# Exponentials read from an SBUF copy of the scores, with scores three steps ahead and four copy buffers

## The chip, the core and the metric

One core of a Trainium2 chip runs the whole program. The metric is device time in microseconds (us), median of the runs, lower is better. Engines: PE is TensorE, DVE is VectorE, ACT is ScalarE, POOL is GpSimd, SP is SyncE. PE accumulates in PSUM, which DVE and ACT read; everything else lies in SBUF.

## The reference, cut to what matters

The part around the change is an attention over clusters, for 2 batches of 8 heads, 768 rows, head width 64:

```python
q_assign = np.argmax(np.einsum('bhsd,hcd->bhsc', q_n, c_n), axis=-1)
k_assign = np.argmax(np.einsum('bhsd,hcd->bhsc', k_n, c_n), axis=-1)
mask = q_assign[:, :, :, None] == k_assign[:, :, None, :]
scores = scale * np.matmul(q, k.transpose(0, 1, 3, 2))
scores = np.where(mask, scores, -1000000000.0)
scores = scores - np.max(scores, axis=-1, keepdims=True)
attn = np.exp(scores)
attn = attn / (np.sum(attn, axis=-1, keepdims=True) + 1e-09)
return np.matmul(attn, v).astype(np.float32)
```

Its output passes a low-rank mix over the tokens with a feed-forward block (512 to 2048 to 512), and then a second block (512 to 1024, a convolution of width 3 as a gate, back to 512). Those follow the attention and are not touched.

## The kernel before

The attention is a software pipeline of 96 steps, one for each tile of 128 query rows by 768 keys (6 tiles to a head, 12 steps to a pair of heads, 8 pairs). `step(n)` is a list of calls, and each engine executes its instructions in exactly the order in which they are called. In step n before the change:

- PE: `s_mm(n + 2)` writes the scores of tile n+2 into a PSUM buffer `sc` (two buffers), in a first part (L351, q and k split in two terms for precision) and a second part (L362, which adds the mask through 16 one-hot rows of `cd`). Then come `pv_mm` of an earlier head (L405, every other step), work for the next pair (below), and `t_mm(n)`, six transposes of the exponentials `e` of tile n (L389) into two PSUM tiles `tr`. `tr`, the one-hot tiles and the mixing tiles share a ring of three PSUM buffers.
- ACT: `t_out(n - 1, 0)` copies one `tr` tile to SBUF (L396), then `s_exp(n + 1)` (L380) makes `e` of tile n+1 from `sc`, with the row's bias `nb` and the row sum.
- DVE: `t_out(n - 1, 1)` copies the other `tr` tile, then `s_max(n + 2)` (L368) reads `sc`, writes the scores times -SCALE into the SBUF tile `e`, and gets their row minimum `nb` out of the same pass. What it writes into `e` is not used: the exponential overwrites it. `e` has three buffers.

For each next pair of heads, PE computes similarities (`sims_wide`, L214) and turns them (`sims_turn`, L228); five DVE operations make the one-hot rows (L245, L247, L249, L251, L253; L249 and L253 have both inputs in SBUF); PE transposes them (`onehot_t`, L260), ACT evicts them and SP puts them into `cd`. POOL loads the operands of a coming head by three DMAs (`load_ops`, L113 to L115) and subtracts (`split_ops`, L125 and L126, both inputs in SBUF). The operand tiles `ab` and `cd` have three buffers for three heads in turn, so that L113, when it loads a head, waits for the last `s_mm` of the head three before. POOL takes all this in its own order too: L113 to L115, then a piece of a weight job (L534, L538 or L515), the small sum L694, L125, L126.

Before the loop, `warm` issues matmuls on zeros; the first steps have no `pv_mm`, and PE waits there for the second half of q's split (`split_first(1, "q")`, whose POOL part is L200). When all heads of batch 0 are done, `mix_t` (step 8 of a pair) brings in eight ACT casts and four DVE subtractions in turn, and its tile too takes a buffer of the PSUM ring.

Of the kernel before, what the change touches and what calls it, by code (L numbers as in the profile page):

```python
# [21 lines left out]
AF = mybir.ActivationFunctionType  # L22
# [11 lines left out]
def tile_kernel(ctx: ExitStack, tc: tile.TileContext, qk, vv, cen, u_w, v_w, w1, w2, win, wout, conv, out):  # L34
    nc = tc.nc
# [3 lines left out]
    NT = S // P  # L39
    HS = S // 2  # L40
# [10 lines left out]
    SCALE = 1.0 / float(D) ** 0.5  # L51
# [15 lines left out]

    att = ExitStack()
    acon = att.enter_context(tc.tile_pool(name="acon", bufs=1))
    a_e = att.enter_context(tc.tile_pool(name="a_e", bufs=3))  # L70
    a_pt = att.enter_context(tc.tile_pool(name="a_pt", bufs=2))
    a_s = att.enter_context(tc.tile_pool(name="a_s", bufs=6))
    a_v = att.enter_context(tc.tile_pool(name="a_v", bufs=2))
# [7 lines left out]
    scores = ExitStack()  # L81
# [69 lines left out]
    def warm(count):  # L151
        for _ in range(count):
            nc.tensor.matmul(idle, busy[:, 0:P], busy, start=True, stop=True)
# [54 lines left out]
    def sims_wide(b, p):  # L208

        pw = ps_t.tile([P, HS], F32, tag="t", name="simw")  # L210
        for half in range(2):
            for i, (r, cb) in enumerate(zip(raw[b, p], (cbq, cbk))):
                o = 2 * NC * (2 * half + i)
                nc.tensor.matmul(pw[o:o + 2 * NC], cb[:, p], r[:, half * HS:(half + 1) * HS], start=True, stop=True)  # L214
        ohst[b, p] = {"pw": pw}

    def sims_copy(b, p):
        sw = a_oh.tile([P, HS], F32, tag="sw", name="sw")
        nc.scalar.copy(sw, ohst[b, p].pop("pw"))
        ohst[b, p]["sw"] = sw  # L220
# [34 lines left out]
    def onehot_t(b, p):  # L255
        oh = ohst[b, p]["oh"]
        pt = ps_t.tile([4 * NC, S], BF16, tag="t", name="oht")
        for t in range(NT):
            g0 = 8 * (t % (NT // 2)) + 4 * (t // (NT // 2))
            nc.tensor.transpose(pt[:, t * P:(t + 1) * P], oh[:, g0:g0 + 4].rearrange("p g c -> p (g c)"), identb)  # L260
        ohst[b, p]["pt"] = pt
# [73 lines left out]
    NQ = B * H * NT  # L335
    NHEAD = B * H
    st = {}
    X = {}

    def head_of(n):  # L340
        b, r = divmod(n, H * NT)
        h, t = divmod(r, NT)
        return b, h, t

    def s_mm_ab(n):
        b, h, t = head_of(n)
        ab, _ = ops[b, h]
        ps = ps_s.tile([P, 2, 512], F32, tag="s", name="sc")
        c0 = t * P
        for f in range(2):  # L350
            nc.tensor.matmul(ps[:, f, 0:HS], ab[:, 0, c0:c0 + P], ab[:, 1, f * HS:(f + 1) * HS], start=True, stop=False)  # L351
        st["s", n] = ps

    def s_mm(n):
        b, h, t = head_of(n)
        if ("s", n) not in st:
            s_mm_ab(n)
        ps = st["s", n]
        _, cd = ops[b, h]
        c0 = t * P  # L360
        for f in range(2):
            nc.tensor.matmul(ps[:, f, 0:HS], cd[0:80, 0, c0:c0 + P], cd[0:80, 1, f * HS:(f + 1) * HS], start=False, stop=True)  # L362

    def s_max(n):
        ps = st["s", n]
        nb = a_s.tile([P, 1], F32, tag="nb", name="nb")
        e = a_e.tile([P, 2, HS], F32, tag="e", name="e")
        nc.vector.tensor_scalar(  # L368
            out=e, in0=ps[:, :, 0:HS], scalar1=-SCALE, scalar2=3e38, op0=ALU.mult, op1=ALU.min, accum_out=nb,
        )  # L370
        st["nb", n] = nb
        st["e", n] = e

    def s_exp(n):
        ps = st.pop(("s", n))
        nb = st.pop(("nb", n))
        if n % NT == 0:
            st["sum", n // NT] = a_s.tile([P, NT], F32, tag="sum", name="sum", bufs=4)
        e = st["e", n]
        nc.scalar.activation(e, ps[:, :, 0:HS], AF.Exp, scale=SCALE, bias=nb, accum_out=st["sum", n // NT][:, n % NT:n % NT + 1])  # L380

    NK = NT // 2

# [14 lines left out]
    def pv_mm(g, k):  # L398

        b, h, _ = head_of(NT * g)  # L400
        if k == 0:
            st["pv", g] = ps_pv.tile([P, HS], F32, tag="pv", name="pv")
        acc, pt = st["pv", g], st["pt", g]
        for i in range(2):
            nc.tensor.matmul(  # L405
                acc[i * D:(i + 1) * D], vts[b, h // 2][:, h % 2, k], pt[:, k, i * NK:(i + 1) * NK].rearrange("p a b -> p (a b)"),
                start=(k == 0), stop=(k == NT - 1),
            )
        if k == NT - 1:
            st.pop(("pt", g))  # L410
# [142 lines left out]
    def mix_t(b):  # L553

        def mm():
            pt = ps_t.tile([P, P], F32, tag="t", name="mt")
            for t in range(NT):
                for c in range(ND):
                    nc.tensor.matmul(
                        pt[c * R:(c + 1) * R], uw[:, t], X[b][:, t, c * P:(c + 1) * P], start=(t == 0), stop=(t == NT - 1))  # L560
            return pt

        def evac(pt):
            for c in range(ND):
                src, cs = pt[c * R:(c + 1) * R], slice(c * P, (c + 1) * P)
                nc.scalar.copy(tts[b][0:R, cs], src)
                nc.vector.tensor_sub(tts[b][R:2 * R, cs], src, tts[b][0:R, cs])
                nc.scalar.copy(tts[b][2 * R:3 * R, cs], src)  # L568

        return mm, evac  # L570
# [30 lines left out]
    def mix_rest(b):  # L601
        for t in range(NT):
            mixing.append(mix_u(b, t))
        for t in range(NT):
            (mixing if b * NT + t < TG or b > 0 else later).append(mix_x(b, t))
# [28 lines left out]

    PLAN = ({2 * k: (2 * k, 2 * k + 1) for k in range(NK)}, NT - 2), ({k: (2 * k, 2 * k + 1) for k in range(NK)}, NK - 1)
    MIX_AT = (4, 6, 8, 10)

    SIM_AT, TURN_AT, ONEHOT_AT, ROWS_AT = 0, (2, 4), ((2, 2, 3, 3, 4), (4, 4, 5, 5, 6)), (5, 7)

    def step(n):  # L640
        pair, s = divmod(n, 2 * NT)
        mix = None
        if s == 8 and pair > 0 and n < NQ:
            b, p = divmod(pair - 1, NP)
            if p == NP - 1:
                mixing.append(mix_t(b))
                mix_rest(b)
        if n == 0:
            sims_wide(0, 1)
            warm(7)  # L650
        if n + 2 < NQ:
            s_mm(n + 2)
        ahead = divmod(pair + 1, NP)
        wide = 0 <= n < NQ and 1 < pair + 1 < B * NP
        rows = 0 <= n < NQ and pair + 1 < B * NP and s == ROWS_AT[pair == 0]
        turn = 0 <= n < NQ and pair + 1 < B * NP and s == TURN_AT[pair == 0]
        if rows:
            onehot_t(*ahead)

        g, r = divmod(n - NT - 1, NT)  # L660
        ks, last = PLAN[g == NHEAD - 1]
        if 0 <= g < NHEAD:
            for k in ks.get(r, ()):
                pv_mm(g, k)
        done = g - 1 if r == 0 else g if g == NHEAD - 1 and r == last + 1 else -1
        if 0 <= done < NHEAD - (r == 0):
            fin_t(done)
        elif mixing and (s in MIX_AT or pair == B * NP - 1):
            mix = mixing.pop(0)
            got = mix[0]()  # L670
        if s == SIM_AT and wide:
            sims_wide(*ahead)
        if turn:
            sims_turn(*ahead)
        if 0 <= n < NQ:
            t_mm(n)
        if 0 <= n - 1 < NQ:
            for i in range(2):
                t_out(n - 1, i)
        if 0 <= n + 1 < NQ:  # L680
            s_exp(n + 1)
        if rows:
            onehot_rows(*ahead)
        if (s == SIM_AT and wide) or n == 0:
            sims_copy(*ahead)
        if n == -1:
            split_first(1, "q")
            split_ops(0, 0, 1, nc.gpsimd)
            load_ops(0, 1, 0)
        if n + 2 < NQ:  # L690
            s_max(n + 2)
        if 0 <= g < NHEAD and r == 0:
            sm = st["sum", g]
            nc.gpsimd.tensor_scalar(out=sm, in0=sm, scalar1=1e-9, scalar2=None, op0=ALU.add)  # L694
        if 0 <= g < NHEAD and r == last:
            fin_a(g)
        if 0 <= done < NHEAD - (r == 0):
            fin_x(done)
        if mix:
            mix[1](got)  # L700
        if 0 <= n < NQ:
            prep(n)

    for n in range(-2, NQ - 2):
        step(n)
    qks.close()
    rp = right.enter_context(tc.tile_pool(name="rp", bufs=3, side="right", reuse_waits="tile"))
    wpc = right.enter_context(tc.tile_pool(name="wpc", bufs=1, side="right", reuse_waits="tile"))
    step(NQ - 2)
    scores.close()  # L710
    ps_a = psums.enter_context(tc.tile_pool(name="ps_a", bufs=1, space=PSUM, reuse_waits="tile"))


# [246 lines left out]
```

## Time and profile before

| what | us |
|---|---|
| runs: median (lowest to highest) | 663.59 (663.41 to 666.61) |
| profiled execution, span from first to last instruction | 662.6 |
| PE busy, share of the span | 647.8, 98% |
| DVE, ACT, POOL busy | 413.8, 326.6, 222.1 |
| attention, from the first score matmul to the last transposes | 10.5 to 246.9 |

The page gives only the span of the profiled execution; the median is 1.0 us above it. Matmuls are pipelined and the ends shown are modelled, so PE's share says little; the starts of its rows tell how fast it goes. The granted clock is 1.00 nearly everywhere, and 0.91 in the stretch from 20 to 40 us.

### The profile page before, as it was taken

To read this page: it belongs to the slowest core of one execution; us is meant where nothing else is said; L and a number is where in the kernel's file an instruction comes from. 1 tells how busy PE (TensorE), PEld (TensorE's weight loads), DVE (VectorE), ACT (ScalarE), POOL (GpSimd) and SP (SyncE) were. 2 spreads that over 40 slices of the span, in tenths; PEclk is the share of its full clock that TensorE was granted. 3 is DMA by queue.
4 is the path that set the end of the run, shared out by engine and by line. 5 is a ranking of instruction groups with operands and counts; after the bars stand their busy time and mean duration, and the time that the engine had idled before them with its cause. 6 is when DMAs were issued, how large, how long until landed. Compare 5 with 4: busy or idle time off the path is not lost.

```text
span 662.6 us, 9733 instructions
## 1 busy us (share of the span) xinstructions
PE 647.8 (98%) x3654; PEld 511.2 (77%) x3654; DVE 413.8 (62%) x737; ACT 326.6 (49%) x621; POOL 222.1 (34%) x222
## 2 busy tenths in 40 slices
PE   9899999999999999999999999999999999999997
PEld 6667676776776766789888888888877888888886
DVE  6868877887888785488326768873177445643400
ACT  5767676766767763243213333331135367753511
POOL 4753435443434012056132333330055624331300
PEclk9999999999999999999999999999999999999999
DMA  7576483745545112023102443340023000000111
GB/s 189 122 170 149 88 204 77 176 103 132 119 116 129 33 49 79 26 72 97 64 0 96 126 128 128 127 135 25 1 74 118 1 0 1 11 24 27 38 48 48
DMA packets 19583, 55.45 MB, mean 84 GB/s; under 512 B 3312, under 2 KB 7024, under 8 KB 19536
## 3 DMA queue, kind: packets, MB, share of 16 engines
q1 hardware_dynamic: 15936, 40.08, 20.0%
q0 software_dynamic: 3600, 14.75, 11.0%
q8 instruction: 29, 0.48, 0.3%
q14 instruction: 18, 0.15, 0.1%
HBM read 50.19 MB, written 3.15 MB: 81 GB/s over the span
## 4 chain that ended last, share of the span: by engine, by line
PE 83%; DVE 11%; issue 3%; ACT 2%; POOL 1%; ACTq 0%; DVEq 0%; POOLq 0%
PE g L849 10%; PE pv L405 9%; PE tr L389 8%; PE h L726 6%; PE h L728 6%; PE h L727 6%; PE a L742 6%; PE a L743 6%; PE a L744 6%; PE sc L351 4%; PE sc L362 4%; PE po L883 3%; PE po L884 3%; PE po L885 3%; DVE e L368 3%
## 5 line engine op out<-in xcount | busy, mean ns | idle before, releaser
L515 POOL TENSOR_TENSOR wl<-wx,wh 128x512 fp32r<-128x512 f32 x48 | 63.2, 1319 | 143.8 <-ACT wh L514 137.9
L368 DVE TENSOR_SCALAR_CACHE_REDUCE e<-sc 128x768 f32<-128x768 f32 x96 | 91.5, 954 | 10.4 <-PE sc L362 9.2
L380 ACT ACTIVATE e<-sc,nb 128x768 f32<-128x768 f32 x96 | 86.9, 905 | 11.2 <-DVE e L368 10.9
L732 DVE SCALAR_TENSOR_TENSOR rl<-h,rh 128x512 fp32r<-128x512 f32 (+1 forms) x52 | 33.6, 647 | 85.8 <-ACT rh L731 85.7
L731 ACT ACTIVATE rh<-h 128x512 fp32r<-128x512 f32 (+1 forms) x52 | 29.3, 563 | 113.1 <-PE h L728 113.1
L389 PEld LDWEIGHTS tr<-identf,e 128*128 128x128 f32 x576 | 65.0, 140 | 25.8 <-issue 6.1
L389 PE MATMUL tr<-identf,e 128*128 128x128 f32 x576 | 80.9, 276 | 0.9 <-ACT tt L568 0.7
L726 PE MATMUL h<-uh,wh 128*128 128x512 f32 (+1 forms) x208 | 78.3, 376 | 1.6 <-DVE rl L732 1.6
L742 PE MATMUL a<-rh,wh 128*128 128x512 f32 (+1 forms) x208 | 78.2, 376 | 0.5 <-DVE xa L758 0.5
L743 PE MATMUL a<-rl,wh 128*128 128x512 f32 (+1 forms) x208 | 77.7, 374 | 0.3 <-DVE rl L732 0.3
L744 PE MATMUL a<-rh,wl 128*128 128x512 f32 (+1 forms) x208 | 77.6, 373 | 0.0
L727 PE MATMUL h<-ul,wh 128*128 128x512 f32 (+1 forms) x208 | 77.6, 373 | 0.0
L728 PE MATMUL h<-uh,wl 128*128 128x512 f32 (+1 forms) x208 | 77.5, 373 | 0.0
L405 PE MATMUL pv<-pt,rv 128*64 128x384 f32 x384 | 74.2, 505 | 0.0
L396 DVE COPY pt<-tr 128x384 f32<-128x384 f32 x96 | 52.9, 552 | 23.6 <-PE tr L389 22.9
L396 ACT COPY pt<-tr 128x384 f32<-128x384 f32 x96 | 46.0, 479 | 42.6 <-PE tr L389 42.6
L514 ACT CAST wh<-wx 128x512 fp32r<-128x512 f32 x48 | 29.7, 618 | 59.9 <-DVE wx L468 59.9
L464 DVE SCALAR_TENSOR_TENSOR wx<-wb,wx 128x512 int32<-128x512 int32 (+3 forms) x52 | 51.6, 993 | 11.6 <-ACT wb L455 9.6
L351 PE MATMUL sc<-ab 128*128 128x384 f32 x192 | 57.2, 380 | 1.4 <-ACT e L380 0.8
L866 POOL TENSOR_TENSOR h<-h,cv 128x768 f32<-128x768 f32 x16 | 29.6, 1850 | 64.8 <-ACT cv L865 64.8
L362 PE MATMUL sc<-cd 80*128 80x384 f32 x192 | 49.5, 339 | 0.0
L726 PEld LDWEIGHTS h<-uh,wh 128*128 128x128 f32 x208 | 39.1, 188 | 9.4 <-DVE rl L732 1.9
(135 smaller groups left out, 1249.3 us busy)
## 6 DMA issues: line engine op xcount, KB each, us to landing
raw<-in_w_dram SPq DMA_DIRECT2D x32, 512.0 KB, 3.7
cd<-in_qk_dram POOLq DMA_DIRECT2D x15, 384.0 KB, 4.3
ab<-in_qk_dram POOLq DMA_DIRECT2D x15, 384.0 KB, 5.4
raw<-in_win_dram SPq DMA_DIRECT2D x8, 512.0 KB, 3.7
raw<-in_wout_dram SPq DMA_DIRECT2D x8, 512.0 KB, 3.7
rv<-in_vv_dram SPq DMA_DIRECT2D x8, 384.0 KB, 3.3
out_dram<-o SPq DMA_DIRECT2D x24, 128.0 KB, 1.8
ab<-in_qk_dram POOLq DMA_DIRECT2D x15, 192.0 KB, 5.7
```

Source lines behind the costliest of these rows:

```text
L351: nc.tensor.matmul(ps[:, f, 0:HS], ab[:, 0, c0:c0 + P], ab[:, 1, f * HS:(f + 1) * HS], start=True, stop=False)
L368: nc.vector.tensor_scalar(out=e, in0=ps[:, :, 0:HS], scalar1=-SCALE, scalar2=3e38, op0=ALU.mult, op1=ALU.min, accum_out=nb,)
L380: nc.scalar.activation(e, ps[:, :, 0:HS], AF.Exp, scale=SCALE, bias=nb, accum_out=st["sum", n // NT][:, n % NT:n % NT + 1])
L389: nc.tensor.transpose(pt[:, k, :], e[:, i, k * P:(k + 1) * P], identf)
L396: (nc.scalar.copy if i == 0 else nc.vector.tensor_copy)(to, st.pop(("t", n, i)))
L405: nc.tensor.matmul(acc[i * D:(i + 1) * D], vts[b, h // 2][:, h % 2, k], pt[:, k, i * NK:(i + 1) * NK].rearrange("p a b -> p (a b)"), start ...
L726: nc.tensor.matmul(ph, wh[:, k, ws], uh[g][:, k, ts], start=(k == 0), stop=False)
L727: nc.tensor.matmul(ph, wh[:, k, ws], ul[g][:, k, ts], start=False, stop=False)
L728: nc.tensor.matmul(ph, wl[:, k, ws], uh[g][:, k, ts], start=False, stop=(k == ND - 1))
L742: nc.tensor.matmul(accs[d][:, 0:n], wh[:, i, ds_], rh, start=(f == 0), stop=False)
L743: nc.tensor.matmul(accs[d][:, 0:n], wh[:, i, ds_], rl, start=False, stop=False)
L744: nc.tensor.matmul(accs[d][:, 0:n], wl[:, i, ds_], rh, start=False, stop=(f == NH - 1))
```

## The change

The exponential now reads the SBUF tile that `s_max` wrote, in place, with scale -1.0. The PSUM buffer `sc` is then done with after `s_max`. Scores lead by three steps in place of two, exponentials by two in place of one, and `e` has four buffers. For the first pair alone, `sims_turn`, the one-hot operations and `onehot_t` are called one step earlier; three warming matmuls are left out there. At the end the pools are closed and opened to match.

```diff
-    a_e = att.enter_context(tc.tile_pool(name="a_e", bufs=3))
+    a_e = att.enter_context(tc.tile_pool(name="a_e", bufs=4))
...
     def s_max(n):
-        ps = st["s", n]
+        ps = st.pop(("s", n))
...
     def s_exp(n):
-        ps = st.pop(("s", n))
...
-        nc.scalar.activation(e, ps[:, :, 0:HS], AF.Exp, scale=SCALE, bias=nb, accum_out=st["sum", n // NT][:, n % NT:n % NT + 1])
+        nc.scalar.activation(e, e, AF.Exp, scale=-1.0, bias=nb, accum_out=st["sum", n // NT][:, n % NT:n % NT + 1])
...
-    SIM_AT, TURN_AT, ONEHOT_AT, ROWS_AT = 0, (2, 4), ((2, 2, 3, 3, 4), (4, 4, 5, 5, 6)), (5, 7)
+    AHEAD = 3
+    SIM_AT, TURN_AT, ONEHOT_AT, ROWS_AT = 0, (2, 3), ((2, 2, 3, 3, 4), (3, 3, 4, 4, 5)), (5, 6)
...
-        if n == 0:
+        if n == 2 - AHEAD:
             sims_wide(0, 1)
-            warm(7)
-        if n + 2 < NQ:
-            s_mm(n + 2)
+            warm(4)
+        if n + AHEAD < NQ:
+            s_mm(n + AHEAD)
...
-        if 0 <= n + 1 < NQ:
-            s_exp(n + 1)
+        if 0 <= n + AHEAD - 1 < NQ:
+            s_exp(n + AHEAD - 1)
...
-        if (s == SIM_AT and wide) or n == 0:
+        if s == SIM_AT and wide:
             sims_copy(*ahead)
-        if n == -1:
+        if n == 2 - AHEAD:
+            sims_copy(0, 1)
+        if n == 1 - AHEAD:
             split_first(1, "q")
...
-        if n + 2 < NQ:
-            s_max(n + 2)
+        if n + AHEAD < NQ:
+            s_max(n + AHEAD)
...
-    for n in range(-2, NQ - 2):
+    for n in range(-AHEAD, NQ - AHEAD):
         step(n)
+    scores.close()
     qks.close()
...
-    step(NQ - 2)
-    scores.close()
+    for n in range(NQ - AHEAD, NQ - 1):
+        step(n)
```

**PE at the start.** PE's rows after the warming matmuls, before the change (numbers are the program's buffer numbers; `e_288` is tile 0, `e_305` tile 1):

```order
L351 MATMUL sc_319<-ab_196 128x384 x2
L362 MATMUL sc_319<-cd_197 128x384 x2
L389 MATMUL tr_324<-identf_119,e_288 128x128 x3
L389 MATMUL tr_328<-identf_119,e_288 128x128 x3
L351 MATMUL sc_338<-ab_196 128x384 x2
L362 MATMUL sc_338<-cd_197 128x384 x2
L389 MATMUL tr_343<-identf_119,e_305 128x128 x3
```

and the same place now:

```order
L351 MATMUL sc_316<-ab_196 128x384 x2
L362 MATMUL sc_316<-cd_197 128x384 x2
L351 MATMUL sc_327<-ab_196 128x384 x2
L362 MATMUL sc_327<-cd_197 128x384 x2
L388 MATMUL tr_332<-identf_119,e_288 128x128 x3
L388 MATMUL tr_336<-identf_119,e_288 128x128 x3
L351 MATMUL sc_344<-ab_196 128x384 x2
```

Two tiles of scores now stand ahead of the first transposes, where one stood.

**PE where a head ends.** PE's rows around the turned similarities of a later pair, before (`ab_299` is one head's operand tile, `ab_398` the next head's):

```order
L351 MATMUL sc_684<-ab_299 128x384 x2
L362 MATMUL sc_684<-cd_300 128x384 x2
L228 MATMUL sim_689<-identf_119,sw_642 128x128 x3
L389 MATMUL tr_693<-identf_119,e_645 128x128 x3
L389 MATMUL tr_697<-identf_119,e_645 128x128 x3
L351 MATMUL sc_713<-ab_299 128x384 x2
L362 MATMUL sc_713<-cd_300 128x384 x2
L405 MATMUL pv_652<-pt_501,rv_214 64x384 x4
```

and now (`ab_414` is the next head's):

```order
L351 MATMUL sc_690<-ab_299 128x384 x2
L362 MATMUL sc_690<-cd_300 128x384 x2
L228 MATMUL sim_695<-identf_119,sw_648 128x128 x3
L388 MATMUL tr_699<-identf_119,e_622 128x128 x3
L388 MATMUL tr_703<-identf_119,e_622 128x128 x3
L351 MATMUL sc_719<-ab_414 128x384 x2
L362 MATMUL sc_719<-cd_415 128x384 x2
L404 MATMUL pv_658<-pt_513,rv_214 64x384 x4
```

The last scores of a head now stand ahead of `sim`, one tile of scores earlier than before; the kinds of rows around it are the same, and so are those on DVE, ACT and POOL in these later pairs.

## Rows read from the trace of the kernel before

**Rows 1.** The page: busy time of each engine, and the chain that ended last by engine.

```profile
PE 647.8 (98%) x3654; PEld 511.2 (77%) x3654; DVE 413.8 (62%) x737; ACT 326.6 (49%) x621; POOL 222.1 (34%) x222
PE 83%; DVE 11%; issue 3%; ACT 2%; POOL 1%; ACTq 0%; DVEq 0%; POOLq 0%
```

**Rows 2.** Timeline of PE, two steps of the middle: start, length, engine, line, operation.

```profile
93.34 0.62 PE L351 MATMUL sc<-ab 128*128 128x384 f32 x2
...
94.25 1.51 PE L405 MATMUL pv<-pt,rv 128*64 128x384 f32 x8
95.69 0.88 PE L389 MATMUL tr<-identf,e 128*128 128x128 f32 x6
96.32 0.59 PE L351 MATMUL sc<-ab 128*128 128x384 f32 x2
...
97.70 0.62 PE L351 MATMUL sc<-ab 128*128 128x384 f32 x2
```

**Rows 3.** Timeline of the start, POOL and PE.

```profile
16.07 0.99 POOL L200 TENSOR_TENSOR ab<-rq,cd 64x384 fp32r<-64x384 f32 x1 [6.86 <-DMA cd<-os]
...
17.68 0.59 PE L351 MATMUL sc<-ab 128*128 128x384 f32 x2 [0.38 <-ACT e L380]
...
19.23 0.62 PE L351 MATMUL sc<-ab 128*128 128x384 f32 x2
...
20.79 0.62 PE L351 MATMUL sc<-ab 128*128 128x384 f32 x2
```

**Rows 4.** Line L249 (ns: least/median/most); timelines of DVE, POOL, PE around the first `oht`.

```profile
L249 DVE TENSOR_TENSOR eq<-eq,iota x9: 258/354/1875, 9.2 to 200.8; 128x384 bf16<-128x384 bf16 x7, 128x192 bf16<-128x192 bf16 x2
...
26.76 1.88 DVE L249 TENSOR_TENSOR eq<-eq,iota 128x384 bf16<-128x384 bf16 x1
...
29.60 0.95 DVE L368 TENSOR_SCALAR_CACHE_REDUCE e<-sc 128x768 f32<-128x768 f32 x1
...
24.70 1.82 POOL L125 TENSOR_TENSOR ab<-rq,cd 64x768 fp32r<-64x768 f32 x1 [2.40 <-DVE e L368]
26.60 1.81 POOL L126 TENSOR_TENSOR ab<-rk,ab 64x768 fp32r<-64x768 f32 x1
...
31.08 0.74 PE L260 MATMUL oht<-identb,oh 128*64 128x128 bf16 x5 [2.19 <-DVE oh L253]
```

**Rows 5.** Stretches (length, PE busy, granted clock, DMA share, GB/s), and PE's timeline.

```profile
31.00:32.00 1.00, 0.92 (x8) 0.50 1.15 234
...
287.00:289.00 2.00, 0.58 (x6) 1.00 0.66 190
...
289.20 0.39 PE L726 MATMUL h<-uh,wh 128*128 128x256 f32 x1 [1.63 <-DVE rl L732]
```

**Rows 6.** Timeline of PE after the mixing of batch 0.

```profile
156.47 0.59 PE L351 MATMUL sc<-ab 128*128 128x384 f32 x2 [0.57 <-issue]
```

**Rows 7.** Timelines where a head ends: third of six pairs; last row, the sixth.

```profile
106.23 0.59 PE L351 MATMUL sc<-ab 128*128 128x384 f32 x2
...
107.92 0.59 PE L351 MATMUL sc<-ab 128*128 128x384 f32 x2
...
109.16 0.59 POOL L113 DMA_DIRECT2D cd<-in_qk_dram  x1 [4.96 <-PE sc L362]
...
112.81 0.56 DVE L253 TENSOR_TENSOR oh<-eq,m 128x384 bf16<-128x384 bf16 x1
...
113.74 1.81 POOL L125 TENSOR_TENSOR ab<-rk,cd 64x768 fp32r<-64x768 f32 x1 [1.15 <-DMA cd<-in_qk_dram]
...
203.67 2.12 POOL L125 TENSOR_TENSOR ab<-rk,cd 64x768 fp32r<-64x768 f32 x1 [1.05 <-DMA cd<-in_qk_dram]
```

**Rows 8.** Groups by line on ACT: out<-in, count | busy us, mean ns of one.

```profile
L380 ACT ACTIVATE e<-sc,nb 128x768 f32<-128x768 f32 x96 | 86.9, 905 | 11.2 <-DVE e L368 10.9
...
L865 ACT ACTIVATE cv<-cv 128x768 f32<-128x768 f32 x16 | 13.6, 850 | 12.5 <-DVE cv L860 12.5
L857 ACT ACTIVATE h<-g 128x768 f32<-128x768 f32 x16 | 13.0, 811 | 3.9 <-PE g L849 2.9 <-DVE gl L873 0.8
```

## Prediction

> **What bounds the kernel now.** The page first: PE is busy 98% of the span and makes up 83% of the chain that ended last, DVE 11%, ACT 2% [rows 1]. Since PE's ends are modelled, I go by the starts of its rows. In the middle of the attention two steps take 97.70 - 93.34 = 4.36 us: `pv` 95.69 - 94.25 = 1.44, the transposes behind it 0.63, and the step without `pv` 97.70 - 96.32 = 1.38 [rows 2]. I read these starts for all 96 steps: from 36 to 150 us every row comes at this pace, but for short waits ahead of `oht` (0.3 us in four pairs; 0.7 in the last two). PE is full there, and a change that lets PE run further ahead of DVE and ACT gains nothing in these steps. What can be gained or lost lies in three places.
>
> At the start, steps without `pv` take 20.79 - 19.23 = 1.56 us instead of 1.38, since `s_mm` waits for the exponential that frees its PSUM buffer (the row at 17.68 names ACT L380) [rows 3]. Then PE stands 2.19 us in front of `oht` at 31.08, because DVE is late with the one-hot rows: its L249 took 1.88 us, of which most is a wait [rows 4]. [...]
>
> After the mixing of batch 0, PE's scores at 156.47 wait 0.57 for an exponential that stood behind the casts in ACT's queue [rows 6].
>
> Ahead of `oht` of the six later pairs DVE is the later one; L253 makes the one-hot rows, and `oht` starts 0.05 to 0.1 after it has ended.
>
> **The change part by part.** *Exponential from SBUF.* On ACT a 128x768 operation from SBUF in place takes 850 ns (L865), one from PSUM 811 (L857): 0.04 us more, so 0.945 in place of 0.905 for L380 [rows 8]; 96 x 0.04 = 3.8 us on ACT. Work that hides it: ACT is 49% busy, and an exponential has now a whole step more until its transposes. I take nothing; without that cover it would be the 3.8. [...]
>
> *More lead.* `s_mm(n + 3)` now waits for `s_max(n + 1)` of two DVE steps ago, and no exponential. With the fourth `e` buffer `s_max(n + 3)` takes the tile of step n-1, whose transposes stand ahead of its own scores on PE: no new wait. In the middle this is worth nothing, since PE is full. After the mixing the wait of 0.57 goes, because that exponential is now done before the casts: **-0.6**.
>
> *The start.* `s_mm(3)` still waits for POOL's L200, which ends at 17.06 [rows 3], and now not for ACT: it starts at about 17.16, not 17.68, with the transposes of tile 0 behind it instead of ahead. From there PE goes at 1.38 a step, plus 0.31 for `sim` (the 1.69 between two scores with `sim` between them [rows 7]) and about 0.5 for a PSUM tile that L247 must free: the scores of tile 9 start at 17.16 + 6 x 1.38 + 0.8 = 26.3 and end at 27.1. Then comes `oht`, and DVE decides. L249 came at 26.76; now it comes earlier by 0.5 (the scores), 0.46 (one copy of `tr` fewer ahead of it) and 3 x 0.18 (DVE waited for PE's slow steps): at 25.3 to 25.6. That lies within POOL's L125, from 24.70 to 26.52. In before, L249 came 0.16 after L126 had begun and ended 0.21 after it; so now it should end 0.21 after L125, at 26.73, before L126 gets on. From there as in before: 0.96 from L249's end to `s_max` at 29.60, 1.48 from there to `oht` [rows 4]. `oht` comes at 29.2 instead of 31.08: 1.9 earlier. But the transposes of tile 6 now stand behind it, 0.6. Gain **1.3** at equal clock.
>
> PE still stands 27.1 to 29.2, 2.1 us. A wait of 2.19 ended in the clock's fall; one of 1.63 in the feed-forward part [rows 5] left it at 1.00. If it falls again it costs about 1.6 (scores and transposes at half speed) in place of 1.4, if not, the 1.4 are saved: -1.1 to -2.7 together. 2.1 is nearer to the 2.19, but the least difference decides; I take the middle, **-1.9**.
>
> *POOL comes earlier too.* This is the cost that I see. L113 loads a head when the last scores of the head three before are through; the row names PE L362, after 4.96 us of waiting. These scores are now one tile of scores earlier, ahead of `sim`: 107.92 - 106.23 = 1.69 us [rows 7]. The same DMA then lands 1.69 earlier, and L125, which waited for nothing else, starts at 112.05 instead of 113.74 and runs to 113.86. DVE's row order and its distance to PE do not change in these pairs, so L253, also with two SBUF inputs, still wants to start at 112.81: in the midst of L125. That such two exclude each other the trace shows in both directions: L249's 1.88 us behind L126 (0.35 in the middle of nine) [rows 4], and L125 at 203.67, which took 2.12 instead of 1.81 when L253 had begun 0.1 before [rows 7]. Behind POOL an operation ends at POOL's end plus its own length less 0.14: L253 at 113.86 + 0.55 - 0.14 = 114.27 in place of 113.37, **0.90 later**, and `oht` with it; PE has nothing else to do.
>
> So for all six pairs, each with its own rows of this kind: 0.41, 0.67 and 0.90 for the first three. In the last three POOL's L515 moves ahead as well, from behind L249 to just ahead of it, since its ACT cast is done in time: L249 ends 0.44 later; L253 then ends 0.54, 0.44 and 0.45 later. Sum **+3.4**. Bounds: 0, if L125 and L515 don't come earlier or DVE gets in first; 5.4, if each pair lost the 0.90. [...]
>
> After `oht`, `pv` covers DVE's lateness for 1.4 us, more than the 0.9. The one-hot rows go on to `cd` by ACT and SP and are now wanted one step sooner; between `oht` and the scores that want them lie at least three steps, over 6 us.
>
> *Sum*: -0.6 - 1.9 + 3.4 = **+0.9**. The profiled execution's span is 662.6 and the median 663.6, 1.0 apart; nothing outside the span changes. Span 663.5, time 664.5.
>
> **The rivals.** *No collision on the port* (20%): POOL's L125 is held by its DMA, or DVE goes first. For it: 1.69 earlier is read from starts, and a landing can slip when other transfers share the engines. Against: L113's row names PE, six times of six. Then -2.5: 661.1; with the clock kept, -3.3: 660.3.
>
> *The first L249 misses its gap* (10%), the slower side: if it comes after 26.52, over 0.9 later than I reckon, it stands behind L126 until 28.63 as before. `oht` is then at 31.08 again, with the transposes of tile 6 behind it: +0.6, with the clock lost as before; +0.6 - 0.6 + 3.4: 667.0. For it: ACT and DVE are nearly as full as PE there (DVE 1.34 a step). Against: the 0.9.
>
> *ACT as the bound of the first seven steps* (3%): an exponential and a copy take about 1.3 there; with 0.04 more still less than 1.38. It decides only from 1.38 on, and 0.1 over it would cost 7 x 0.1 = 0.7: 665.2.
>
> **How the numbers follow.** Forecast as summed: 67%, with its own range 663.6 to 665.5, from the clock. 0.5% of the time is 3.3 us, about what a measurement here tells from no change: faster is below 660.3, slower above 666.9. Faster: about half of the rival without collision, 9%. Slower: most of the missed gap and a little of the forecast with longer delays, 9%. Same: 82%. The range, 661.0 to 666.6, leaves out the missed gap and the half of the first rival with the clock kept.
>
> **What would show it.** Right: L125 in the six pairs begins 1.7 us earlier against `sim`, L253 lasts over 0.9 us in the first pairs, and PE waits 0.7 to 1.2 us ahead of `oht` for it; the first `oht` at about 29; no wait of PE for L379 anywhere (the exponential's line now). L379's mean near 945 ns. Wrong: L253 at 0.55 us throughout and `oht` waits as before (first rival); L249 still near 1.9 us (second); or steps of the middle that take less than 4.36 us a pair, which would mean that PE was not full there and the time falls by more than all of this.

## The result, and the profile after

Slower by 1.1%: 671.51 us median (668.64 to 673.98, 5 executions) against 665.66 (663.41 to 666.61, 5) of the kernel before beside it, ratio 1.011, 95% interval 1.0079 to 1.014. The forecast was 664.5, with 661.0 to 666.6 as the range. The profiled execution of the changed kernel took 668.64 and is the quickest of the five; the others ran at a mean granted clock of 0.989 to 0.997, it at 0.997. Beside the experiments below the kernel before has medians of 663.5 to 663.7 (27, 34 and 28 executions), so 665.66 lies high; against these the change is 1.012.

The page, beside [rows 1]: the span is 4.1 us longer, and PE is busy no longer than before. PE waits more.

```profile
span 666.7 us, 9706 instructions
PE 646.1 (97%) x3651; PEld 510.0 (76%) x3651; DVE 419.6 (63%) x737; ACT 329.3 (49%) x621; POOL 221.2 (33%) x222
```

I took the starts of the transposes of each step in both traces and subtracted. The difference changes mainly at few places:

| term, us of span | forecast | measured |
|---|---|---|
| start | -1.9 | -0.6 |
| six `oht` of the later pairs | 0.41, 0.67, 0.90, 0.54, 0.44, 0.45 = +3.4 | 0.94, 0.47, 0.98, 0.56, 0.53, 1.88 = +5.4 |
| after the mixing of batch 0 | -0.6 | -0.66 |
| sum | +0.9 | +4.1 |

(The start: +0.12 at step 9. With the longer lead one more tile of scores is done by then, and PE gets that back at the end of the attention, where the difference falls by 0.72. Left out are a slow drift of -0.35 over the attention and a step of +0.4 at 302 us in the feed-forward part, which about cancel.)

Timelines of POOL, DVE and PE round the third and the sixth later pair, to set beside [rows 7]:

```profile
113.44 1.81 POOL L125 TENSOR_TENSOR ab<-rk,cd 64x768 fp32r<-64x768 f32 x1 [0.98 <-DMA cd<-in_qk_dram]
115.33 2.02 POOL L126 TENSOR_TENSOR ab<-rq,ab 64x768 fp32r<-64x768 f32 x1
114.20 1.47 DVE L253 TENSOR_TENSOR oh<-eq,m 128x384 bf16<-128x384 bf16 x1
115.73 0.47 PE L260 MATMUL oht<-identb,oh 128*64 128x128 bf16 x5 [1.23 <-DVE oh L253]
...
202.87 1.27 POOL L514 TENSOR_TENSOR wl<-wx,wh 128x512 fp32r<-128x512 f32 x1 [0.95 <-issue]
204.59 1.81 POOL L125 TENSOR_TENSOR ab<-rk,cd 64x768 fp32r<-64x768 f32 x1
206.48 1.80 POOL L126 TENSOR_TENSOR ab<-rq,ab 64x768 fp32r<-64x768 f32 x1
203.47 0.88 DVE L249 TENSOR_TENSOR eq<-eq,iota 128x384 bf16<-128x384 bf16 x1
206.80 1.90 DVE L253 TENSOR_TENSOR oh<-eq,m 128x384 bf16<-128x384 bf16 x1
208.75 0.47 PE L260 MATMUL oht<-identb,oh 128*64 128x128 bf16 x5 [2.04 <-DVE oh L253]
```

In the third pair L253 started inside L125 and ended at 115.67, 0.42 behind L125's end at 115.25: the forecast's own formula (GpSimd's end, plus 0.55, less 0.14). In the sixth L249 first lost 0.53 beside the weight split L514; L253 then came at 206.80, after L125 was through and 0.32 after L126 had begun, and stood behind L126.

The start, to set beside [rows 4]: POOL, DVE, PE, and the queue of SP that carries the one-hot rows into `cd`; then two stretches with the granted clock at 0.50.

```profile
25.19 1.83 POOL L125 TENSOR_TENSOR ab<-rq,cd 64x768 fp32r<-64x768 f32 x1 [2.84 <-DVE pt L395]
27.10 1.81 POOL L126 TENSOR_TENSOR ab<-rk,ab 64x768 fp32r<-64x768 f32 x1
25.75 1.49 DVE L249 TENSOR_TENSOR eq<-eq,iota 128x384 bf16<-128x384 bf16 x1
29.08 0.55 DVE L253 TENSOR_TENSOR oh<-eq,m 128x384 bf16<-128x384 bf16 x1
29.69 0.85 PE L260 MATMUL oht<-identb,oh 128*64 128x128 bf16 x6 [2.52 <-DVE oh L253]
31.64 2.41 SPq L274 DMA_DIRECT2D cd<-os  x4
...
30.00:31.00 1.00, 1.00 (x9) 0.83 (x7) 0.98 (x3) 0.60 (x3) 0.68 (x2) 0.50 0.96 252
31.00:32.00 1.00, 1.00 (x6) 1.00 (x5) 0.00 (x0) 1.00 (x3) 0.00 (x0) 0.50 1.20 258
```

L249 did end 0.22 behind the end of L125, as forecast (0.21), and did not wait for L126. But L125 itself began at 25.19 and not at 24.70: the load of `cd`, which it reads, landed at 25.06 for 24.57, 0.13 ahead of L125 both times (the row's bracket names the DVE instruction before). So `oht` came at 29.69, not 29.2. The clock fell again, to 0.50 over 30 to 32 us.

The exponential's line against [rows 8]: 938 ns for 905, 0.033 more each (forecast 0.04), and PE waits for it nowhere.

```profile
L379 ACT ACTIVATE e<-e,nb 128x768 f32<-128x768 f32 x96 | 90.0, 938 | 11.2 <-DVE e L368 10.7
```

### The profile page after: what moved, and what is told of

It reads as the page before. It is cut to its first block, busy times and chain, and to the rows that moved or that the text cites. A ratio compares the mean times of both kernels' runs of the same rounds, so it can differ in the third digit from the quotient of the medians.

```text
span 666.7 us, 9706 instructions
## 1 busy us (share of the span) xinstructions
PE 646.1 (97%) x3651; PEld 510.0 (76%) x3651; DVE 419.6 (63%) x737; ACT 329.3 (49%) x621; POOL 221.2 (33%) x222
## 4 chain that ended last, share of the span: by engine, by line
PE 81%; DVE 11%; issue 3%; ACT 2%; POOL 1%; DMA 0%; ACTq 0%; POOLq 0%; DVEq 0%
PE g L852 10%; PE pv L404 9%; PE tr L388 8%; PE h L729 6%; PE h L731 6%; PE h L730 6%; PE a L746 5%; PE a L745 5%; PE a L747 5%; PE sc L351 4%; PE sc L362 4%; PE po L886 3%; PE po L888 3%; PE po L887 3%; DVE e L368 2%
## 5 line engine op out<-in xcount | busy, mean ns | idle before, releaser
L514 POOL TENSOR_TENSOR wl<-wx,wh 128x512 fp32r<-128x512 f32 x48 | 62.9, 1311 | 150.2 <-ACT wh L513 147.2
L379 ACT ACTIVATE e<-e,nb 128x768 f32<-128x768 f32 x96 | 90.0, 938 | 11.2 <-DVE e L368 10.7
L735 DVE SCALAR_TENSOR_TENSOR rl<-h,rh 128x512 fp32r<-128x512 f32 (+1 forms) x52 | 33.7, 648 | 85.5 <-ACT rh L734 85.4
L388 PE MATMUL tr<-identf,e 128*128 128x128 f32 x576 | 82.3, 278 | 1.4 <-ACT tt L567 0.7
L404 PE MATMUL pv<-pt,rv 128*64 128x384 f32 x384 | 72.8, 498 | 0.0
L362 PE MATMUL sc<-cd 80*128 80x384 f32 x192 | 49.7, 341 | 0.0
```

The source lines that it names most:

```text
L379: nc.scalar.activation(e, e, AF.Exp, scale=-1.0, bias=nb, accum_out=st["sum", n // NT][:, n % NT:n % NT + 1])
L388: nc.tensor.transpose(pt[:, k, :], e[:, i, k * P:(k + 1) * P], identf)
L404: nc.tensor.matmul(acc[i * D:(i + 1) * D], vts[b, h // 2][:, h % 2, k], pt[:, k, i * NK:(i + 1) * NK].rearrange("p a b -> p (a b)"), start ...
```

## The experiments

The theory: VectorE's one-hot instructions and GpSimd's subtractions shut each other out, and the longer lead sets them on top of each other. (The texts on record say "port" for this; what the two share no run shows.) Rivals: the exponential from SBUF or the new order of engines costs by itself; TensorE's clock falls for reasons of its own at the start. Ratios are to the kernel before, run beside each group (medians 663.71, 663.58 and 663.53).

**e1, GpSimd held behind L249.** A copy of one element per partition on GpSimd reads what L249 wrote, so that the loads, and all behind them, come after it. (Added lines move the later line numbers: L260 is L265 here, L362 is L367, and L514 is L519.)

```diff
+        nc.gpsimd.tensor_copy(gate, ohst[b, p]["eq"][:, 0, 0:1])
...
+                    if part == 2 and nxt > 1:
+                        hold(b, p)
```

> The changed kernel, with one tiny POOL copy per later pair that reads eq after L249, ahead of L113: POOL's loads, weight split and subtractions of the pair come behind L249, and L125 some 87 against an oht at 85, so behind L253 too. Theory P (POOL comes earlier with the scores' lead and L253 and L249 wait for it at the port): L249 0.35 and L253 0.55 us in all six pairs, PE's waits ahead of oht back to 0.3 (four pairs) and 0.7 (two); of the changed kernel's 666.7 us span 5.4 go: 661.3, ratio to before 0.996 to 1.002. Rival A (the exponential from SBUF, or the longer lead itself, is what costs): span 666 to 667, ratio 1.008 or more.

Measured: 668.23 us, ratio 1.0055 (1.0035 to 1.0075), not the 0.996 to 1.002 expected; the span, 666.5, is the one that rival A gave, so that the pairs have to decide. In the first three pairs the loss is gone (difference to before -0.1 to -0.4). The last three lost 3.2, 1.0 and 1.0. Their cause is in the timeline of the fourth, DVE, POOL, PE, with two stretches behind it (the granted clock, 0.56 and 0.50, is the third number from the end, as in [rows 5]):

```profile
141.00 2.19 DVE L253 TENSOR_TENSOR oh<-eq,m 128x384 bf16<-128x384 bf16 x1
141.46 1.31 POOL L519 TENSOR_TENSOR wl<-wx,wh 128x512 fp32r<-128x512 f32 x1
143.25 0.47 PE L265 MATMUL oht<-identb,oh 128*64 128x128 bf16 x5 [1.94 <-DVE oh L253]
...
144.00:146.00 2.00, 2.00 (x10) 0.69 (x7) 0.53 (x2) 1.00 (x2) 1.93 (x2) 0.56 0.68 111
146.00:147.00 1.00, 1.00 (x7) 1.00 (x5) 0.00 (x0) 0.66 (x3) 1.00 (x1) 0.50 0.45 89
```

The weight split L519 had been moved off L249 and onto L253. Behind the wait of 1.94 the granted clock fell to 0.50, which made that pair the dearest. So the theory held in the three pairs that the copy freed, and in the others the remedy only moved the collision.

**e2, the exponential from SBUF alone.** The leads, the three `e` buffers and the first pair's numbers as before; `s_max` frees the scores' PSUM buffer.

```diff
-        nc.scalar.activation(e, ps[:, :, 0:HS], AF.Exp, scale=SCALE, bias=nb, accum_out=st["sum", n // NT][:, n % NT:n % NT + 1])
+        nc.scalar.activation(e, e, AF.Exp, scale=-1.0, bias=nb, accum_out=st["sum", n // NT][:, n % NT:n % NT + 1])
```

> The kernel before with the exponential alone changed: it reads the SBUF copy in place, and PSUM is free after the maximum; leads, buffers and the first pair as before. Theory P: POOL's loads come as before, no collision: L253 at 0.55, L379's line near 938 ns, ratio 0.998 to 1.002. Rival A: ACT's 0.033 us per exponential (3.2 us in all) shows: ratio 1.004 or more.

Measured: 663.96, ratio 0.9999 (0.9978 to 1.0021). A slow exponential as the cause is refuted: no loss builds up from step to step. The profile gains 2.2 at the start and 0.65 after the mixing, and, against the expectation, loses 1.6 in each of the last two pairs. There L125 comes first, by 0.08 and 0.03 us (timelines of POOL and DVE, fifth pair):

```profile
170.65 1.80 POOL L125 TENSOR_TENSOR ab<-rk,cd 64x768 fp32r<-64x768 f32 x1 [0.83 <-DMA cd<-in_qk_dram]
172.52 2.02 POOL L126 TENSOR_TENSOR ab<-rq,ab 64x768 fp32r<-64x768 f32 x1
...
170.73 2.13 DVE L253 TENSOR_TENSOR oh<-eq,m 128x384 bf16<-128x384 bf16 x1
```

**e3, seven warming matmuls again** (`warm(4)` back to `warm(7)` in the changed kernel).

> The changed kernel with seven warming matmuls ahead of tile 2's scores in place of four. Theory P: no difference to the changed kernel, ratio to before 1.008 to 1.014. Rival C (clock falls in the first 20 us of some executions, as PE stands idle from 16.2 to 17.2, make the median larger than the profile shows): the clock of all executions is 0.997, the median 2 us or more lower: ratio 1.005 to 1.008.

Measured: 672.68, ratio 1.0128 (1.0097 to 1.0158). The start is no better (+0.45 at step 9), so the matmuls left out are not the cause. Its profile shows what the changed kernel's own did not: long `oht` waits in the last two pairs with the clock falling right behind. Stretches round both, and PE's rows there:

```profile
178.00:179.00 1.00, 0.12 (x2) 0.12 (x3) 1.00 (x2) 0.00 (x0) 0.41 (x1) 0.81 0.00 0
179.00:181.00 2.00, 2.00 (x12) 1.48 (x14) 1.17 (x3) 0.99 (x1) 0.00 (x0) 0.50 0.00 0
...
213.00:215.00 2.00, 2.00 (x8) 0.68 (x4) 0.54 (x2) 0.80 (x1) 0.00 (x0) 0.50 0.03 8
...
178.88 0.74 PE L260 MATMUL oht<-identb,oh 128*64 128x128 bf16 x5 [2.29 <-DVE oh L253]
...
212.25 0.47 PE L260 MATMUL oht<-identb,oh 128*64 128x128 bf16 x5 [2.07 <-DVE oh L253]
```

These two pairs cost 3.7 and 3.6 us in e3.

**e4, the first pair held too.** e1, and the first pair's split and loads behind its L249.

```diff
+                    if part == 2:
+                        hold(b, p)
...
+            if s == (1 if nxt > 1 else 4):
                 split_ops(b, p, 0, nc.gpsimd)
```

> As the first, and in the first pair POOL's subtractions and loads also behind L249. Theory P: L249 at 0.35 there too, first oht 1.1 us earlier, near 28.6; span 660.2 if the clock falls for 3.4 us again, 658.8 if not; ratio 0.992 to 0.999, a little faster than before. Rival A: 665 to 666, ratio 1.006 or more.

Measured: 668.86, ratio 1.0066 (1.0045 to 1.0086). The first `oht` came at 28.61, 1.1 earlier than in the changed kernel, but the difference of -2.3 at step 8 was +1.5 at step 9: PE stood waiting up to 36.62 for the new one-hot rows on their way into `cd`, and the two matmuls there took 0.98 us, where the same two took 0.59 in e8 (the mean granted clock of this execution was 0.995):

```profile
36.62 0.98 PE L367 MATMUL sc<-cd 80*128 80x384 f32 x2 [2.03 <-DMA cd<-os]
```

So an earlier `oht` did not make an earlier start.

**e5, everything held behind L253.** The copy reads `oh`, and the weight splits that would go out between are called behind it; the loads stay.

```diff
+        nc.gpsimd.tensor_copy(gate, ohst[b, p]["oh"][:, 0, 0:1])
...
-            nc.gpsimd.tensor_sub(lo, x, hi)
+            behind(lambda: nc.gpsimd.tensor_sub(lo, x, hi))
...
+                    if part == 4 and nxt > 1:
+                        hold(b, p)
+                        st["held"] = False
+                        while late:
+                            late.pop(0)()
```

> The change with one tiny GpSimd copy that reads the one-hot rows (so GpSimd stands until L253 is done), and behind it both of GpSimd's works that met VectorE's one-hot instructions in the six later pairs: the weight split (L514, L537 of the changed kernel) and L125. The loads L113 to L115 stay where they were. Port theory: no L249 or L253 is stretched any more (0.35 and 0.55 us in all six), none of the six waits for oht grows, so the span loses the 5.4 us that they had added to the changed kernel and keeps its other terms (start about 0, mixing -0.65, tail -0.75): 661 to 661.5 us, time 663.0 to 663.5, ratio to before 0.997 to 1.000. Rival, that the loss comes from the exponential two steps ahead itself (VectorE and ScalarE in another order): it stays, 666 to 668. Clock theory (the clock falls behind a long wait of TensorE for oht): no fall behind a later pair, at most the one in the first.

Measured: 663.11, ratio 0.9991 (0.9978 to 1.0004); the loss is gone. (The profiled span, 662.7, is above the 661 to 661.5 expected: in that execution the granted clock was also at 0.50 from 11 to 14 us, and the start lost 1.7.) The groups by line (ns: least, median, most; the most of L249 is the first pair's, which is not held):

```profile
L253 DVE TENSOR_TENSOR oh<-eq,m x9: 357/553/555, 9.8 to 204.2; 128x384 bf16<-128x384 bf16 x7, 128x192 bf16<-128x192 bf16 x2
L249 DVE TENSOR_TENSOR eq<-eq,iota x9: 257/353/1418, 9.1 to 201.4; 128x384 bf16<-128x384 bf16 x7, 128x192 bf16<-128x192 bf16 x2
```

Ten of eleven executions lie between 662.8 and 664.6, where the changed kernel's five spread over 5.3.

**e6, e2 with e5's hold.**

> The exponential from the SBUF copy alone (leads, buffers and first-pair numbers as before; e2) with the same hold as in e5. e2's span lost 1.6 us in each of the fifth and sixth later pairs, where L125 started within 0.1 us of L253. Port theory: both come back, so the span is 659 to 659.5 us if the clock holds in the first pair as in e2's profile (start -2.7, mixing -0.65), 660.5 to 661 if it falls there as before; time 661 to 662.8, ratio 0.995 to 0.999. Rival (no port loss in e2, another cause there): as e2, ratio 1.000.

Measured: 661.88, ratio 0.9964 (0.9946 to 0.9981): a version quicker than both kernels. The two losses of e2 are gone, L253 is 0.55 throughout. Four executions at a mean clock of 0.998 and more took 660.3 to 660.6, the seven at 0.995 to 0.997 took 661.6 to 663.6.

**e7, only L125 held.** e5 without the second edit.

> The change with the hold ahead of L125 alone; the weight splits stay where they were, ahead of L249. Port theory, from the rows of the changed kernel: the three pairs where L125 met L253 come back (first, third and sixth: 0.95, 1.0 and 1.4 to 1.9 us), the second comes back by the 0.4 us of its L253, the fourth and fifth keep their 0.5 each (L249 stays at 0.88 beside the weight split): span 662.4 to 663.2, time 664.3 to 665.1, about 1.3 us above e5. If the split, not L125, were the main loss, it would stay above 665.

Measured: 664.90, ratio 1.0015 (1.0000 to 1.0030), 1.8 above e5 (expected 1.3). L253 is at 0.55 or 0.56 in all six pairs; L249 stays at 0.88 in three, and these cost 0.53 each. So the collision with L125 and L126 is the larger part, that with the weight splits some 1.6 of the 5.4 us.

**e8, the first wait filled.** e5, with six idle matmuls where PE stands in front of the first `oht`.

```diff
         if rows:
+            if pair == 0:
+                warm(6)
             onehot_t(*ahead)
```

> e5 with six idle matmuls (warm) put on TensorE just ahead of the first pair's onehot_t, where it stands for about 3 us; they compute nothing that is used. Clock theory (the clock falls because TensorE stands still there): the clock stays at 1.00 behind the first oht, the start term comes out at -1.3 to -2.7 in place of about 0, span 658.8 to 660.2, time 660.7 to 662.1. Rival (the fall has another cause, or comes a little later anyway as in e4): the span is that of e5 or above, since the six matmuls take some 1 us in a wait.

Measured: 663.16, ratio 0.9996 (0.9983 to 1.0009). The clock stays at 1.00 behind the first `oht`, as it does in e7 without the matmuls, and still the span is 661.3, not the 658.8 to 660.2 expected: a wait stands further on that the slow clock had hidden. PE's timeline, and the transfers issued from 28 to 38 us (KB each, us to landing):

```profile
29.73 0.52 PE L265 MATMUL oht<-identb,oh 128*64 128x128 bf16 x6 [1.50 <-DVE oh L253]
...
36.97 0.59 PE L367 MATMUL sc<-cd 80*128 80x384 f32 x2 [1.25 <-DMA cd<-os]
...
cd<-os SPq DMA_DIRECT2D x4, 48.0 KB, 4.7
```

These are the scores of tile 12, the first that need the new one-hot rows, now asked for in step 9 instead of 10. The other profiles with the longer lead in which the clock stayed up behind `oht` have the same wait: 1.12 (e1), 1.29 (e3) and 0.94 (e7). The rows' transfers took 2.1 us in the kernel before and 4.2 in the changed one:

```profile
cd<-os SPq DMA_DIRECT2D x4, 48.0 KB, 2.1
```

```profile
cd<-os SPq DMA_DIRECT2D x4, 48.0 KB, 4.2
```

**e9, other loads first.** e8 with the first pair's order on GpSimd changed: the loads of the next head ahead of a split (at 17.2 instead of 20.8 us), and the loads of the head after it, in flight beside the rows in e8, behind the one-hot rows (at 33.7 instead of 28.9).

```diff
+            load_ops(0, 1, 0)
             split_ops(0, 0, 1, nc.gpsimd)
-            load_ops(0, 1, 0)
...
-                    if part == 4 and nxt > 1:
+                    if part == 4:
                         hold(b, p)
+                        if nxt == 1:
+                            split_ops(b, p, 0, nc.gpsimd)
+                            load_ops(b, p, 1)
```

> e8 with GpSimd's first-pair order changed: the loads for the next pair's first head (L113 to L115) go ahead of the split of the present pair's second head, so they land some 5 us earlier; their own split (L125, L126) and the next loads stand behind the first one-hot rows. Theory R (the start's gain is lost because the four small transfers of the one-hot rows into cd, 2.1 us each in the kernel before and 4.2 to 4.7 us in the changed one and e8, run beside those loads and so land at 36.2 to 36.9 us however early they start, and tile 12 of the scores waits for them a step earlier than before): the row transfers take 2 to 2.5 us again and land by 34, the 1.25 us wait of the cd matmul of tile 12 goes, span 659.8 to 660.3, time 661.6 to 662.2. Rival (that wait is only where another lateness shows, of VectorE or ScalarE in the first steps): the span stays within 0.3 of e8's 661.3.

Measured: 666.43, ratio 1.0031 (1.0000 to 1.0062): 3.3 slower than e8, against the expected gain. Half of it came out as expected: the rows took 2.1 us, tile 12 waited for nothing (35.61), and up to step 11 the kernel was 1.4 ahead of e8. Then the loads pushed back ran beside the raw tiles of the pair after, and PE stood in front of the similarities for them; behind that the granted clock fell to 0.50, and both together cost 5.4:

```profile
cd<-os SPq DMA_DIRECT2D x4, 48.0 KB, 2.1
...
35.61 0.52 PE L367 MATMUL sc<-cd 80*128 80x384 f32 x2
...
45.47 0.81 PE L214 MATMUL simw<-rq,cbq 128*32 128x384 f32 x2 [2.08 <-DMA rq<-in_qk_dram]
47.14 0.51 PE L214 MATMUL simw<-rk,cbk 128*32 128x384 f32 x1 [0.87 <-DMA rk<-in_qk_dram]
```

**e10, e6 with the filled wait.**

> e6 (the exponential from the SBUF copy alone, held) with the six idle matmuls in the first pair's wait, as in e8. Clock theory: executions of e6 at a mean clock of 0.998 and more took 660.3 to 660.6 us and those at 0.995 to 0.997 took 661.6 to 663.6; with the wait filled most stand in the first group: median 660.2 to 660.8, ratio to before 0.9945 to 0.996. Rival (the clock falls for another cause): median as e6, 661.9.

Measured: 661.12, ratio 0.9961 (0.9934 to 0.9988), above the 660.2 to 660.8 expected and not told apart from e6 by its interval. All twelve executions are at a clock of 0.999 or 1.000, where seven of e6's eleven were at 0.995 to 0.997: with the wait filled the clock kept up here. But only six took 660.3 to 660.7; the other six, at the same clock, took 661.6 to 662.0. What parts these two groups is open; the profiled execution is of the first.

**e11, the first pair's numbers of before** (`TURN_AT` 4, `ONEHOT_AT` 4 4 5 5 6, `ROWS_AT` 7) in e8.

> e8 with the first pair's numbers of the kernel before (TURN_AT 4, ONEHOT_AT 4 4 5 5 6, ROWS_AT 7), that part of the change undone. What the prediction took for granted (the first one-hot 1.4 to 1.9 us earlier shortens the start by as much): 1.3 us slower than e8, span 662.6. Theory R (the row transfers land at about 36 to 37 us either way): the first oht at 30.5 to 31 us, the row transfers take 2 to 2.5 us and land within 0.7 us of e8's, and the span is within 0.7 us of e8's 661.3.

Measured: 667.30, ratio 1.0045 (1.0014 to 1.0076). Both expectations missed. Up to step 11 it is 1.0 ahead of e8 although its `oht` came 1.6 later (31.32): the rows, sent later, took 2.2 us, and tile 12 waited 0.32. Then SP's queue, 1.5 later with all that follows the rows, brought the raw tiles of the pair after only at 47.05, and PE stood for them. That queue was as late in the kernel before (the last of these tiles sent at 37.13, 37.05 here), and the tile landed at 44.12. There GpSimd's next loads went out behind it, at 37.61, and here ahead of it, at 36.38; that this order makes the difference is argued, not shown. Behind the wait the granted clock was at 0.50. Four of the twelve executions took 663.2 to 664.9, the other eight, the profiled one among them, 667.1 to 669.2:

```profile
35.95 0.58 PE L367 MATMUL sc<-cd 80*128 80x384 f32 x2 [0.32 <-DMA cd<-os]
...
47.19 0.82 PE L214 MATMUL simw<-rk,cbk 128*32 128x384 f32 x1 [2.63 <-DMA rk<-in_qk_dram]
```

## Why the prediction was wrong

**Middle, mixing, exponential: right.** PE was full in the middle and gained nothing there (the waits ahead of `oht` read as 0.3 us are 0.21 to 0.25); the wait after the mixing went (-0.66 for -0.6); ACT's longer exponential cost nothing, by e2 too.

**The collision: right, its size too small.** L125 did come onto L253, by loads that were 1.2 to 1.9 us earlier against PE, and the weight split onto L249. Held apart (e5), all 5.4 us came back; held in part (e7), that part. In four pairs (the first three and the sixth) L253 took 0.97 to 1.90 us for 0.55 and ended 0.41 or 0.42 behind the subtraction that it had met; in e1's fourth pair (last section) L253 began first and still ended last. So the runs show that the two make each other wait, but not what they share.

The step that failed is the sum +3.4, and the bound beside it, "5.4, if each pair lost the 0.90". For the last two pairs it counted L249's lateness alone and put L126, weighed for the first L249 only, at nothing. Rows of before in the sixth pair, DVE and POOL:

```profile
203.57 0.55 DVE L253 TENSOR_TENSOR oh<-eq,m 128x384 bf16<-128x384 bf16 x1
...
205.87 1.83 POOL L126 TENSOR_TENSOR ab<-rq,ab 64x768 fp32r<-64x768 f32 x1
```

L126 begins 0.08 behind L125's end (203.67 and 2.12). With L125 1.69 earlier and at its 1.81, L126 begins at 203.87, and L253, 0.44 later by L249, at 204.01: inside L126, and by the prediction's own formula 2.0 late, not 0.45. The sixth pair did just that (1.88). The fifth pair's rows (L253 at 173.82, L125 at 173.92) give the same 2.0, and it escaped by luck: its L125 came only 1.26 earlier, so that L253 met L125's last 0.13 us and got in ahead of L126 (0.53). The first pair lost 0.94 for 0.41 because there, too, L125 came only 1.21 earlier and ended later against L253; the other three came within 0.2. With L125 and L126 where they stood, the formula gives all six to 0.02. So the sum hung on tenths of a microsecond in the landing of a load, and the honest bound of a pair was a whole subtraction (L253 took 2.13 for 0.55 in e2) on top of L249's 0.5: 2.1. In all the pairs cost 5.4 for 3.4, which is 2.0 of the 3.2 us missed in span.

**The start: -0.6 for -1.9.** Half a microsecond is `oht` at 29.69 for 29.2, by a load's landing. The rest is the clock, taken half-way: it fell, as it had before. The 1.4 us reckoned for the fall of before are read from its chain, at a granted clock of 0.50 from 31 to 34 us: `pv` behind `oht` took 2.57 us where 1.44 is usual, and `oht` itself 0.74 [rows 4] where it takes 0.47 at a clock of 1.00:

```profile
31.82 2.57 PE pv L405 x8
...
37.31 1.44 PE pv L405 x8
```

Had the clock not fallen, the -2.7 would not have come either: in e1, e3, e7 and e8 it stayed at 1.00 behind `oht`, and the start was worth 0.3 to 0.9. The step that failed here is a sentence: "between `oht` and the scores that want them lie at least three steps, over 6 us". In the changed kernel the rows needed 6.9 (29.69 to their landing at 36.59), in e8 7.1, as they now share the DMA engines with the loads of a head. Over 33 to 35 us the DMA share, second from the end, is 1.15 where it was 0.68 (before, then changed):

```profile
33.00:35.00 2.00, 2.00 (x13) 0.91 (x9) 0.00 (x0) 0.36 (x3) 1.93 (x2) 0.71 0.68 113
...
33.00:35.00 2.00, 2.00 (x14) 1.00 (x14) 0.97 (x2) 0.17 (x1) 1.93 (x2) 1.00 1.15 202
```

e9 takes this wait away, e11 most of it, and both show the next transfer behind it. Where the clock stays up, the start of the kernels with the longer lead is thus set by what the DMA engines bring in, up to 47 us; in the changed kernel's profile and in e5's the slow clock hides it.

**Span and median: 1.0 was too little.** The executions of this record, the profiled one here among them (668.64 and 666.7), are 1.7 to 1.9 longer than their spans. By that the profiled execution of the kernel before took about 664.4 (an estimate), and the prediction's 1.0 set its span against the median of others, 663.59. That is 0.9 more of the 7.0 missed in time.

**The clock elsewhere: not in the sum.** From the profile alone the time would be 668.6; the median is 2.9 above. The other four executions have no profile. e1 and e3 show the granted clock at 0.50 right behind `oht` waits of 1.94 to 2.29 in later pairs, at a cost above 1 us each, and with these waits gone (e5) the spread went too. That the four ran so is argued from these, not shown. Not every such wait ends so: the sixth pair of the profiled execution waited 2.04 and kept its clock (1.00 from 208 to 212 us). Of the eighteen waits of PE of 1.94 to 2.67 us in all thirteen profiles, eleven are followed by a clock of 0.50 and seven are not, so the length of the wait alone does not tell.

Of the rivals, "no collision on the port" and "ACT as the bound" are refuted. The one on the slower side was named for the first pair of the run; its mechanism came true in the sixth later one.

## What to carry to other kernels

When a change frees a buffer earlier, ask what the engine that waited for it will now run beside, and order the two by data (a copy of one element per partition is enough) instead of by luck: that, with the weight splits put behind the copy, turned 1.011 into 0.9991. Where two instructions shut each other out, bound the loss by the length of all that can stand ahead in the other's queue, not by today's distance between them. And where the gain is an earlier start, follow the data to its last transfer: here the first transfer of the one-hot rows was sent 1.4 us earlier and landed 0.9 later.

## What the runs showed that was not expected

- Two GpSimd subtractions 0.07 to 0.08 us apart let a waiting VectorE instruction in between (L253 in the first three pairs, 0.97 to 1.50 us), but one that comes 0.32 after the second has begun stands for all of it (1.90 us for 0.55).
- In e1's fourth pair L253 began 0.46 before L519 and still ended 0.42 behind it, as if it had come second. Why is open.
- The four transfers of 48 KB took 2.1 us each where GpSimd's loads of a head were nearly through (before) or only just being sent (e9), and 4.2 to 4.7 in the midst of these loads of 192 and 384 KB (changed, e8). Sent 1.4 us earlier, the first landed 0.9 later (36.22 for 35.32).
- Six idle matmuls in a wait kept the granted clock at 0.999 and above in twelve of twelve executions (e10) and in nine of eleven (e8), where without them it was 0.995 to 0.997 in seven of eleven (e6) and in seven of eleven (e5).
